# An attention and MLP kernel on one core: the last batch's first MLP product by a seven-product scheme, variances by ScalarE squares, and a new order

## The chip, the core and the metric

One NeuronCore of a Trainium2 chip. The kernel is one program, launched once, with inputs and output in HBM. The metric is the device time of an execution in microseconds; the median of several runs counts. TensorE (PE) multiplies, VectorE (DVE), ScalarE (ACT) and GpSimd (POOL) do the elementwise work, and SyncE's queue (SP) issues nearly all transfers. TensorE writes to PSUM, eight banks of 512 fp32 columns in 128 partitions; GpSimd works on SBUF alone.

## The reference

Four batches of 768 positions, eight heads of 64. The first half is a causal block-sparse attention; the second mixes its output and runs an MLP:

```python
# attention, per batch and head (S = 768, D = 64, blocks of 64 keys)
k_rep = mean of k over each block                     # 12 blocks
gate  = q @ k_rep.T, causal by block                   # S x 12
sel   = top 3 blocks of gate, and the own block
attn  = softmax(q @ k.T / 8 over the selected, causal) # S x S
x     = attn @ v                                       # heads side by side: 768 x 512

# mixing and MLP, per batch
X     = fft(fft(x, axis=seq), axis=model)
u     = x + real(X)
un    = (u - mean(u)) / sqrt(var(u) + 1e-6)            # over the 512 columns
ch    = relu(un @ w_ch1) @ w_ch2                       # 512 -> 2048 -> 512
out   = u + ch
```

## The kernel before

The work is cut into some 1160 steps, and one hand-written string, `ORDER`, lists them. Each word is a step, `name:arguments@place`; a tilde ahead of it picks the other of two engines. A loop at the end goes through the words and emits each step's instructions; nothing is reordered after that. Each engine therefore runs its own instructions in the order of the list and waits by semaphores for its inputs. `@place` names the buffer that a step's result takes, above all one of four PSUM slots of two banks each.

Attention runs over 16 pairs of heads (pair P belongs to batch P // 4): loads `Lq`, `Lk`, `Lv`, scores `s` (six tiles a pair), exponentials `e` on ACT, causal masks `d` on POOL, `v` (probabilities times values) on TensorE, the normalised result `x` on DVE. Then, per batch: folds `fs`, `fd`, `f`, `fe` (they halve the transforms), the first transform `y` with its copies `ty` and `tr`, the second transform `m`, and `u`, which adds x on DVE and collects the row sums (`m_u`).

Per batch and tile of 128 rows follow the statistics, the normalising and the transpose:

- `bn` (`n_stats`, lines 747 and 748): bn_stats over 512 columns and bn_aggr, on DVE;
- `nv` (`n_guess`): a first guess of 1/sqrt of the variance, on DVE, for two tiles at a time; `nr` (`n_newton`): Newton steps in small POOL instructions;
- `xu` (`m_x`, lines 704 and 707): centring and scaling to fp16, one tile on ACT and one on DVE;
- `un` (`t_copy`, line 742): two transposing transfers on SP's queue, which put the two tiles into `unT`. Later `od` steps (line 832, results to HBM) share this queue.

The MLP's first product is `w` (`w1_mm`, lines 801 and 803): sixteen steps a batch, each with four weight tiles of 128 x 128 against 768 columns of `unT`, as 512 and 256. `r` (`w1_relu`, lines 811 and 813) takes the relu of all 768 columns from PSUM to fp16 `hT`, on ACT or DVE.

The second product is plain for batches 0 and 1 (`c`, line 820, with `o` at line 826). For batches 2 and 3 (`W7`) it is already a seven-product scheme: instead of eight products of half matrices it forms seven of sums of halves. `T` (`w2_comb`) builds four sums of w2's quarters; `S` (`h_comb`) four sums of the quarters of `hT`, 32 steps a batch, 128 x 384 fp16, through the helper `tt` at line 250; `p` (`w7_mm`, line 879) is one product for 128 rows, eight matmuls of 256 columns; `po` (`w7_o`, line 886) scales the partial result and adds it to u on DVE. Seven products in three row groups make 21 `p` and 21 `po` a batch. Partial products that go to the same place are added up in the PSUM bank, which each `po` reads in between.

The order at the end before the change: `c` of batch 1 interleaved with the scores of pairs 14 and 15; `w:2`; the transforms of batch 3 in between; `p:2`, then `w:3`, then `p:3` and the last `od`.

Of the kernel before, what the change touches and what calls it, by code (L numbers as in the profile page):

```python
# [19 lines left out]
S = 768  # L20
# [84 lines left out]

ORDER = """
# [24 lines left out]
Lv:7@1 bn:0,1 r:0,0 s:7,1@3 Lk:10@0 r:0,10 ks:9 d:7,3 w:0,11@0 e:7,1 qc:8@1 s:7,2@1 kh:9 ~r:0,11  # L131
# [25 lines left out]
e:13,2 gl:14 s:13,4@2 f:2,2 w:1,3@0 ~fe:2,0 e:13,4 gm:14@2 d:13,2 ~fe:2,3 f:2,3 d:13,1 kh:15
w:1,14@3 f:2,1 r:1,7 K:14 qc:15@1 s:12,4@2 r:1,14 ~fe:2,2 f:2,0 w:1,0@1 e:12,4 nv:1 s:13,0@3 fe:2,1
~r:1,3 y:2,0@2 e:13,0 ~r:1,0 d:13,0 s:12,2@0 d:13,3 pg:2 g:15@3 e:12,2 d:13,4 y:2,1@1 gt:15 vc:13
tr:2,0 d:12,0 s:12,3@3 Lv:14@0 gu:15 nr:1 gx:15 ty:2,0 c:1,0,0@0 go:15 gl:15 e:12,3 ~ty:2,1 v:13@2  # L160
~tr:2,1 ~qs:15 m:2,0@3 d:12,3 x:13 d:12,2 qs:14 m:2,2@1 gm:15@3 kc:15 u:2,0@0 c:1,1,0 d:12,4 d:12,5
bn:2,0 vc:12 s:14,1@2 u:2,2@2 s:14,0@3 K:15 c:1,0,1 e:14,0@0 bn:2,4 e:14,1 bn:2,1 s:14,2@1 d:14,0
bn:2,5 s:14,4@3 e:14,2 c:1,1,1 e:14,4 ~vc:14 v:12@2 o:1,1 o:1,0 od:1,1 s:15,0@1 nv:2,2 od:1,0
s:15,5@3 c:1,4,0@0 e:15,5@1 e:15,0 xu:2,2 x:12 d:15,0 s:15,3@3 d:14,2 s:14,3@1 nv:2,0 un:2,2 e:15,3
c:1,4,1 fs:13,1 e:14,3 xu:2,0 d:15,3 fs:13,0 d:14,4 s:14,5@2 d:14,1 m:2,1@3 o:1,4 e:14,5 d:15,5
s:15,1@1 od:1,4 u:2,1@1 d:14,3 s:15,2@2 e:15,1 c:1,5,0 bn:2,2 e:15,2 d:15,1 d:14,5 bn:2,3 s:15,4@3
d:15,2 v:14@1 nv:2,1 e:15,4 ~xu:2,1 c:1,5,1 d:15,4 un:2,1 nr:2 v:15@2 o:1,5 T:2 od:1,5 c:1,2,0@3
un:2,0 x:14 c:1,2,1 x:15 fs:12,1 fs:12,0 c:1,3,0 fs:14,1 fs:14,0 fs:15,1 fs:15,0 fd:14,1 fd:15,1
# [28 lines left out]
def kernel(  # L197
# [546 lines left out]

    def n_stats(b, kt):
        bst = spool.tile([128, 6], FP, tag="bst", name=f"bst{kt}_{b}", bufs=4)
        nc.vector.bn_stats(out=bst, in_=u_t[b, kt // 2][:, kt % 2, :])
        nc.vector.bn_aggr(out=st_t[b][0][:, kt, :], in_=bst)

    def n_guess(b, kp=None):  # L750
        if b in W7:

            if len(st_t[b]) == 3:
                st_t[b].append([spool.tile([128, NST], FP, tag=n, name=f"{n}_{b}")
                                for n in ("vr", "t2")])
            k = slice(2 * kp, 2 * kp + 2)
            mv, g, nm, vr = [t[:, k] for t in (*st_t[b][0:3], st_t[b][3][0])]
# [6 lines left out]
            nc.vector.scalar_tensor_tensor(out=nm, in0=mv[:, :, 0], scalar=-1.0, in1=g,  # L764
                                           op0=ALU.mult, op1=ALU.mult)
# [68 lines left out]
    w2t, h_s, rt_t = [], {}, {}  # L834

    def w2_comb(n):
        if not w2t:
            w2t.extend(apool.tile([128, PT_W], F16, tag=f"pt{m}", name=f"w2t{m}", bufs=1)[:, 0:4096]
                       .rearrange("p (n i c) -> p n i c", n=2, c=256) for m in range(2))
        lo, hi = slice(0, 256), slice(256, 512)  # L840
        for i0, i1 in ((0, 8),):
            b11, b21, b12, b22 = [w2_sb[:, r + i0:r + i1, c] for c in (lo, hi) for r in (0, 8)]
            t = [w2t_at(m, i0, i1) for m in range(4)]
            in0, in1 = ((b12, b11), (b22, t[0]), (b22, b12), (b21, t[1]))[n]
            tt(t[n], in0, in1, ALU.subtract)

    def w2t_at(m, i0, i1):
        return w2t[m // 2][:, m % 2, i0:i1, :]

    def h_comb(b, i, n):  # L850
# [5 lines left out]
        def a(r, c):  # L856
            return h_t[b, i + 8 * (c - 1)][:, 384 * (r - 1):384 * r]
# [3 lines left out]
        tt(s[:, n, :], in0, in1, ALU.subtract if n else ALU.add)  # L861

    def w7_mm(b, n, st):
# [86 lines left out]
    def ind_slot0():  # L950
# [61 lines left out]
```

## Time and profile before

| | |
|---|---|
| Runs | 277.74, 280.2, 277.95 us; median 277.95 |
| Profiled execution | 277.79 us, its span 276.1 us |
| Granted TensorE clock | 1.00 |
| TensorE busy | 267.9 us (97%), 2660 matmuls |
| VectorE busy | 221.5 us (80%), 683 instructions |
| ScalarE busy | 178.3 us (65%), 243 |
| GpSimd busy | 107.4 us (39%), 304 |
| Read from HBM, written | 28.55 MB, 6.29 MB |

The span runs from the first to the last instruction; the execution's own time is 1.7 us longer. Rows of groups give the code line, engine, operation, result and inputs with shape and type, the number, and behind the first bar the busy time and the mean duration of one instruction in ns; behind the second bar stands the idle time of the engine just ahead of them and what ended it. Rows of the timeline give start and duration in us. A waiting row reads "who waited <- for whom: us in total, times, longest". Matmuls are pipelined, so a row's duration is longer than its distance to the next one; distances are the better price. Names such as `L801` are the lines of the kernel above; `L250` and `L239` are helpers that many steps share.

### The profile page before, as it was taken

The page shows a single profiled execution, that of the slowest core. Times are in us where ns is not written, and L with a number is a line of the kernel's source. Part 1 is how long each engine was busy: PE and PEld are TensorE (multiplying, and loading weights), DVE is VectorE, ACT ScalarE, POOL GpSimd, SP SyncE. Part 2 cuts the span into 40 slices and gives each one's busy share as a digit, 9 for nine tenths or more (in the row PEclk, how much of TensorE's full clock was granted, in tenths as well). Part 3 has the DMA queues.
Part 4 walks back from the last instruction along what each step waited for, and adds up shares of the span by engine and source line. Part 5 has one row for each costly group of instructions (what it writes and reads, how often), then busy time and mean ns, then how long its engine had stood idle before and what let it go on. Part 6 is the DMA issues. An engine that isn't in the chain of part 4 may idle for free.

```text
span 276.1 us, 7004 instructions
## 1 busy us (share of the span) xinstructions
PE 267.9 (97%) x2660; PEld 181.2 (66%) x2660; DVE 221.5 (80%) x683; ACT 178.3 (65%) x243; POOL 107.4 (39%) x304
## 2 busy tenths in 40 slices
PE   8899989999999999999999999999999999999995
PEld 4566766765576565666665755655766888666884
DVE  1888999998789889899789797879999894307883
ACT  3799999969999759978799687802546310274100
POOL 5155927634783476405976691520100011000000
PEclk9999999999999999999999999999999999999999
DMA  8999999998799999479471202351100412300025
GB/s 190 271 229 235 186 233 207 180 153 151 134 174 189 168 188 194 115 124 234 119 149 29 57 2 78 77 105 51 38 2 0 59 19 68 127 0 2 0 112 194
DMA packets 121138, 33.47 MB, mean 121 GB/s; under 512 B 113616, under 2 KB 118160, under 8 KB 121104
## 3 DMA queue, kind: packets, MB, share of 16 engines
q1 hardware_dynamic: 115872, 28.43, 48.1%
q0 software_dynamic: 3664, 4.19, 9.8%
q10 hardware_dynamic: 1568, 0.39, 0.6%
q8 instruction: 21, 0.34, 0.5%
q14 instruction: 13, 0.11, 0.1%
HBM read 28.55 MB, written 6.29 MB: 126 GB/s over the span
## 4 chain that ended last, share of the span: by engine, by line
PE 81%; DVE 6%; ACT 5%; POOL 2%; issue 2%; SPq 2%; DMA 1%; DVEq 0%; ACTq 0%; POOLq 0%
PE h L801 19%; PE cw L879 13%; PE c L820 12%; PE h L803 9%; PE sc L532 7%; PE av L567 5%; PE tp L320 2%; ACT pt L549 2%; PE yp L639 2%; PE sc L527 2%; PE mx L672 2%; SPq L742 2%; PE mx L673 2%; PE sc L539 1%; PE warmps L914 1%
## 5 line engine op out<-in xcount | busy, mean ns | idle before, releaser
L549 ACT ACTIVATE pt<-sc 128x1024 f16<-128x1024 f32 (+1 forms) x96 | 83.4, 925 | 12.1 <-PE sc L532 8.1
L801 PE MATMUL h<-unT,w 128*128 128x512 f16 x256 | 84.6, 379 | 0.3 <-DMA unT<-x 0.3
L803 PE MATMUL h<-unT,w 128*128 128x256 f16 x256 | 69.7, 272 | 0.0
L813 ACT ACTIVATE hT<-h 128x768 f16<-128x768 f32 x50 | 39.4, 811 | 41.1 <-PE h L803 40.7
L555 POOL TENSOR_SCALAR_AFFINE_SELECT pt<-pt 128x256 f16<-128x256 f16 x96 | 37.4, 413 | 21.0 <-ACT pt L549 19.9
L820 PE MATMUL c<-w_sb,hT 128*128 128x512 f16 x192 | 44.5, 379 | 0.0
L801 PEld LDWEIGHTS <-w 128*128 128x128 f16 x256 | 25.0, 98 | 29.7 <-issue 1.4
L820 PEld LDWEIGHTS <-hT 128*128 128x128 f16 x192 | 18.3, 98 | 20.3 <-issue 0.5
L253 POOL TENSOR_SCALAR_AFFINE_SELECT qk<-mt 32x160 f16<-32x160 f16 x72 | 23.9, 353 | 18.2 <-DVE mt L504 16.7
L803 PEld LDWEIGHTS <-w 128*128 128x128 f16 x256 | 25.0, 98 | 3.6
L532 PE MATMUL sc<-qk 96*128 96x512 f16 (+3 forms) x144 | 26.1, 305 | 0.0
L567 PEld LDWEIGHTS <-pt 128*128 128x128 f16 x672 | 22.3, 97 | 3.2 <-ACT pt L549 0.7
L567 PE MATMUL av<-v,pt 128*128 128x65 f16 x672 | 23.2, 193 | 0.3 <-ACT pt L549 0.3
L253 POOL TENSOR_SCALAR_AFFINE_SELECT qk<-q 64x768 f16<-64x768 f32 (+1 forms) x15 | 12.3, 822 | 22.8 <-ACT q L239 15.3
L886 DVE SCALAR_TENSOR_TENSOR u<-cw,rt,u 128x256 f32<-128x256 f32 x35 | 16.6, 480 | 4.7 <-PE cw L879 4.1
L879 PEld LDWEIGHTS <-s 128*128 128x128 f16 x192 | 18.8, 98 | 2.2
L532 PEld LDWEIGHTS <-qk 96*128 96x128 f16 x144 | 13.1, 98 | 7.8
L811 DVE TENSOR_SCALAR hT<-h 128x768 f16<-128x768 f32 x14 | 13.3, 956 | 4.0 <-PE h L803 3.9
L879 PE MATMUL cw<-w2t,s 128*128 128x256 f16 x144 | 16.4, 273 | 0.0
L250 DVE TENSOR_TENSOR s<-hT,hT 128x384 f16<-128x384 f16 x16 | 5.4, 354 | 13.4 <-ACT hT L813 13.3
L250 DVE TENSOR_TENSOR x<-av,rcp 128x768 f16<-128x768 f32 x16 | 15.3, 958 | 0.6
L879 PEld LDWEIGHTS <-hT 128*128 128x128 f16 x144 | 14.1, 98 | 2.0
(155 smaller groups left out, 457.2 us busy)
## 6 DMA issues: line engine op xcount, KB each, us to landing
nat<-in_v_dram SPq DMA_DIRECT2D x16, 384.0 KB, 4.6
out_dram<-u SPq DMA_DIRECT2D x20, 256.0 KB, 2.4
nat<-in_k_dram SPq DMA_DIRECT2D x36, 96.0 KB, 3.4
nat<-in_q_dram SPq DMA_DIRECT2D x36, 96.0 KB, 2.9
nat<-in_q_dram SPq DMA_DIRECT2D x13, 192.0 KB, 3.7
nat<-in_k_dram SPq DMA_DIRECT2D x13, 192.0 KB, 3.9
w_sb<-in_moe_w_ch_dram POOLq DMA_DIRECT2D x2, 1024.0 KB, 11.2
w<-in_moe_w_ch_dram POOLq DMA_DIRECT2D x2, 768.0 KB, 7.1
```

What stands on the lines that cost most here:

```text
L250: (eng or nc.vector).tensor_tensor(out=out, in0=in0, in1=in1, op=op)
L253: nc.gpsimd.affine_select(out=out, in_=in_, pattern=[[0, i] for i in n], base=0, channel_multiplier=0, compare_op=ALU.is_ge, fill=0.0)
L532: nc.tensor.matmul(ps[:, e, co:co + q1 - q0], qk[0:96, e, 1, 128 * jt:128 * jt + 128], qk[0:96, e, 0, q0:q1], start=True, stop=True)
L549: nc.scalar.activation(out=d["pt"][:, o:o + 2 * n].rearrange("p (e c) -> p e c", e=2), in_=d["sc", i][:, :, 0:n], func=AF.Exp, scale=0.125)
L555: nc.gpsimd.affine_select(out=dg, in_=dg, pattern=[[0, 2], [1, 128]], base=0, channel_multiplier=-1, compare_op=ALU.is_ge, fill=0.0)
L567: nc.tensor.matmul(av[:, e, 66 * st:66 * st + 65], pt[:, co:co + 128], vv[:, e, jt, 0:65], start=(cnt == 0), stop=(cnt == 20))
L801: nc.tensor.matmul(hp[:, 0:512], w1s, unT[:, dt, 0:512], start=(dt == 0), stop=(dt == NDT - 1))
L803: nc.tensor.matmul(hp[:, 512:768], w1s, unT[:, dt, 512:768], start=(dt == 0), stop=(dt == NDT - 1))
L813: nc.scalar.activation(out=hT, in_=hp, func=AF.Relu)
L820: nc.tensor.matmul(c_ps[b, g[0]][:, st - g[0], :], h_t[b, it][:, 128 * st:128 * (st + 1)], w2_sb[:, it, :], start=(it == 0), stop=(it == N ...
L879: nc.tensor.matmul(o, x, y, start=(i == 0 and W7_FIRST[n]), stop=(i == 7), skip_group_check=True)
L886: nc.vector.scalar_tensor_tensor(out=o, in0=c_ps[b, "w", st][:, W7_BANK[n], 0:256], scalar=rt_t[b][:, kt:kt + 1], in1=o, op0=ALU.mult, op1 ...
```

## The change

Three things change.

First, batch 3's first product. `unT` is split into halves of its contraction (two pairs of 128-row tiles) and of its columns (384 each), w1 into halves of its contraction and of its 2048 outputs. `W6 = 3` names the batch. `wa` (`w6_comb`) builds four sums of w1's quarters in twelve pieces, on DVE or POOL, in buffers of the attention that are free by then; `ub` (`w6_tcomb`) four sums of the quarters of `unT` on DVE. Then, for eight groups i of outputs, seven products `k:i,n` (`w6_mm`), each two matmuls of 384 columns into one of two banks of a PSUM slot. The sums wander through PSUM: `zc` (`w6_keep`) copies the first bank's partial sum to SBUF in fp32 three times (ACT or DVE), `za` (`w6_add`) adds the second bank and such a copy on DVE into an fp32 tile, `zm` (`w6_max`) takes its relu to fp16 on POOL or ACT, and `zr` (`w6_relu`) takes the first bank's last state directly. Sixteen `w`, sixteen `r` of 768 columns become 56 `k`, 24 `zc`, 24 `za`, 24 `zm` and 8 `zr` of 384.

Second, the statistics of batches 2 and 3: `mn` turns the row sums into negative means on DVE, `sq` lets ACT square u minus the mean and collect the sum, and `nv` takes the variance from that. The twelve `bn` of these batches fall away.

Third, the order from the end of batch 0's output on is new, engines included: a few `S` and the `wa` go to POOL (tilde), copies and relus change sides, the first `k` stand among the last `p:2`, and the first `p:3` among the last `k`. Ahead of that place one neighbouring pair of steps on different engines is exchanged. In `w7_mm`, `w7_o` and `h_comb` the row halves of batch 3 are taken the other way round (`half`).

```diff
+W6 = 3
+W6_A = ((0, 2), (2, 4), (4, 8))
...
+    def n_mean(b, kp):
+        sm = st_t[b][2][:, 2 * kp:2 * kp + 2]
+        nc.vector.tensor_scalar(out=sm, in0=sm, scalar1=-1.0 / DM, scalar2=None, op0=ALU.mult)
+
+    def n_square(b, kt):
+        nc.scalar.activation(out=x_t[b][:, kt, :], in_=u_t[b, kt // 2][:, kt % 2, :], func=AF.Square,
+                             bias=st_t[b][2][:, kt:kt + 1], accum_out=st_t[b][0][:, kt, 1:2])
...
-            nc.vector.tensor_scalar(out=vr, in0=mv[:, :, 1], scalar1=1e-6, scalar2=None, op0=ALU.add)
+            nc.vector.tensor_scalar(out=vr, in0=ss, scalar1=1.0 / DM, scalar2=1e-6, op0=ALU.mult, op1=ALU.add)
...
-            nc.vector.scalar_tensor_tensor(out=nm, in0=mv[:, :, 0], scalar=-1.0, in1=g,
-                                           op0=ALU.mult, op1=ALU.mult)
+            tt(nm, nm, g, ALU.mult)
...
+    def w6_comb(n, r):
...
+        in0 = (lambda: a(1, 0), lambda: w6_sum(0, i0, i1), lambda: a(0, 0), lambda: a(0, 1))[n]()
+        in1 = (lambda: a(1, 1), lambda: a(0, 0), lambda: a(1, 0), lambda: w6_sum(1, i0, i1))[n]()
+        tt(w6_sum(n, i0, i1), in0, in1, ALU.subtract if n else ALU.add, pick(nc.vector, nc.gpsimd))
...
+    def w6_tcomb(n):
+        in0 = (lambda: w6_b(0, 1), lambda: w6_b(1, 1), lambda: w6_b(1, 1), lambda: w6_b(1, 0))[n]()
+        in1 = (lambda: w6_b(0, 0), lambda: w6_t(0), lambda: w6_b(0, 1), lambda: w6_t(1))[n]()
+        tt(w6_t(n), in0, in1, ALU.subtract)
...
+    def w6_mm(i, n):
+        if (i, "p") not in w6:
+            w6[i, "p"] = pst([128, 2, 512], f"k{i}_{W6}")
+        o = w6[i, "p"][:, W7_BANK[n], 0:384]
...
+        for d in range(2):
+            nc.tensor.matmul(o, x[:, d, :], y[:, d, :], start=(d == 0 and W7_FIRST[n]), stop=(d == 1),
+                             skip_group_check=True)
+
+    def w6_keep(i, j):
+        conv(pick(nc.scalar, nc.vector), w6_copy(i, j), w6[i, "p"][:, 0, 0:384], None)
+
+    def w6_relu(i):
+        hp, h = w6[i, "p"][:, 0, 0:384], w6_h(i, 1, 0)
+        if pick(0, 1):
+            nc.vector.tensor_scalar(out=h, in0=hp, scalar1=0.0, scalar2=None, op0=ALU.max)
+        else:
+            nc.scalar.activation(out=h, in_=hp, func=AF.Relu)
+
+    def w6_add(i, j):
+        tt(w6_tmp(i, j), w6[i, "p"][:, 1, 0:384], w6_copy(i, (0, 2, 1)[j]), ALU.add)
+
+    def w6_max(i, j):
+        h, t = w6_h(i, *((0, 0), (1, 1), (0, 1))[j]), w6_tmp(i, j)
+        if pick(0, 1):
+            nc.scalar.activation(out=h, in_=t, func=AF.Relu)
+        else:
+            nc.gpsimd.tensor_scalar(out=h, in0=t, scalar1=0.0, scalar2=None, op0=ALU.max)
...
-            tt(t[n], in0, in1, ALU.subtract)
+            tt(t[n], in0, in1, ALU.subtract, pick(nc.vector, nc.gpsimd))
...
-        tt(s[:, n, :], in0, in1, ALU.subtract if n else ALU.add)
+        tt(s[:, n, :], in0, in1, ALU.subtract if n else ALU.add, pick(nc.vector, nc.gpsimd))
```

The order around the new product, cut:

```diff
+S:2,6,1 po:2,1,1 p:2,1,2 po:2,1,0 S:2,5,1 xu:3,2 p:2,2,1 un:3,2 S:2,2,2 po:2,1,2 p:2,2,0 ...
+p:2,3,2 S:2,6,2 ub:2 k:0,0@2 S:2,3,3 k:0,1 po:2,3,2 p:2,3,1 S:2,5,3 zc:0,0 S:2,4,3 po:2,3,0 p:2,4,2
+za:0,0 po:2,3,1 ~zm:0,0 p:2,4,0 wa:1,2 p:2,4,1 ...
+... k:1,0@0 zc:2,0 p:2,5,0 za:2,0 k:0,6 po:2,5,0 k:2,2 za:0,1 k:1,1 zc:2,1 p:2,6,0 zc:1,0 zm:0,1 zr:0
+za:1,0 k:2,3 k:2,5 po:2,6,0 k:1,2 zm:1,0 ~zc:2,2 od:2,3 k:0,4 ~wa:2,2 zc:1,1 k:3,0@1 ...
+k:6,6 za:4,2 ~zm:3,2 k:7,2 zm:7,0 k:5,6 za:6,1 zc:7,1 p:3,0,2@2 zm:4,2 za:5,1 zr:6 S:3,3,0 zr:5 k:7,3
+S:3,3,2 ~zm:5,1 k:7,5 S:3,4,0 po:3,0,2 k:6,4 zc:7,2 ~S:3,4,1 k:5,4 za:6,2 k:7,6 ...
```

More of the change, by code (lines that the diff above doesn't have):

```diff
@@ L157 @@
[L157 to L168, printed above, removed]
@@ L836, in w2_comb, with w2t_tiles @@
+    w2t, w2p, h_s, rt_t = [], [], {}, {}
+    def w2t_tiles():
+        if not w2p:
+            w2p.extend(apool.tile([128, PT_W], F16, tag=f"pt{m}", name=f"w2t{m}", bufs=1)
+                       for m in range(2))
+            w2t.extend(t[:, 0:4096].rearrange("p (n i c) -> p n i c", n=2, c=256) for t in w2p)
     def w2_comb(n):
-        if not w2t:
-            w2t.extend(apool.tile([128, PT_W], F16, tag=f"pt{m}", name=f"w2t{m}", bufs=1)[:, 0:4096]
-                       .rearrange("p (n i c) -> p n i c", n=2, c=256) for m in range(2))
+        w2t_tiles()
@@ L844, in w2_comb, with half @@
             in0, in1 = ((b12, b11), (b22, t[0]), (b22, b12), (b21, t[1]))[n]
-            tt(t[n], in0, in1, ALU.subtract)
+            tt(t[n], in0, in1, ALU.subtract, pick(nc.vector, nc.gpsimd))
     def w2t_at(m, i0, i1):
         return w2t[m // 2][:, m % 2, i0:i1, :]
+    def half(b, r):
+        return 1 - r if b == W6 else r
     def h_comb(b, i, n):
@@ L866, in w7_mm @@
         o = c_ps[b, "w", st][:, W7_BANK[n], 0:256]
-        rows, low = slice(128 * st, 128 * st + 128), slice(128 * (st + 3), 128 * (st + 4))
+        rows, low = [slice(128 * k, 128 * k + 128) for k in (st + 3 * half(b, 0), st + 3 * half(b, 1))]
         lo, hi = slice(0, 256), slice(256, 512)
@@ L883, in w7_o @@
         r, c = W7_OUT[n]
-        kt = st + 3 * r
+        kt = st + 3 * half(b, r)
         o = u_t[b, kt // 2][:, kt % 2, 256 * c:256 * c + 256]
```

144 lines of the change are left out of this document (109 added, 35 removed).

## The prediction

> **What bounds the kernel now.** I read the page's head and its forty slices first, then TensorE's own waits from 120 us on, then busy time by stretch.
>
> ```profile
> span 276.1 us, 7004 instructions
> PE 267.9 (97%) x2660; PEld 181.2 (66%) x2660; DVE 221.5 (80%) x683; ACT 178.3 (65%) x243; POOL 107.4 (39%) x304
> PE   8899989999999999999999999999999999999995
> ```
>
> ```profile
> PE av L567 <- ACT pt L549: 0.3, 1, 0.3
> PE h L801 <- DMA unT<-x: 0.3, 1, 0.3
> ```
>
> ```profile
> 134.50:214.29 79.79, 79.22 (x715) 50.42 (x713) 68.59 (x203) 50.53 (x67) 32.46 (x89) 1.00 0.25 59
> 214.29:233.50 19.21, 19.21 (x178) 17.21 (x176) 15.57 (x44) 2.62 (x4) 2.54 (x11) 1.00 0.27 43
> 233.50:250.00 16.50, 16.50 (x104) 9.92 (x102) 2.62 (x4) 7.57 (x10) 0.00 (x0) 1.00 0.17 64
> 250.00:276.10 26.10, 22.80 (x196) 18.95 (x194) 19.01 (x53) 2.55 (x4) 0.00 (x0) 1.00 0.23 82
> ```
>
> In the windows the columns are PE, PEld, DVE, ACT, POOL, the granted clock (1.00), DMA. The order list changes in earnest only from about 134.5 us on (the steps listed behind that place are 138.3 us of TensorE, counted back from the last drain at 272.8 us, which the chain further down shows). From there TensorE has no gap but two of 0.3 us and the 3.3 us behind its last matmul. So the kernel is TensorE's column count, and any column taken out after 134.5 us is time, as long as the other engines follow. Between 233.5 and 250 us they are nearly idle: DVE 2.6 of 16.5 us, ACT 7.6, POOL nothing. That stretch is the last batch's first product, which is what the change replaces.
>
> **What is removed.** The price of a column comes from two neighbouring rows of TensorE's timeline: 24 matmuls of 256 columns from 230.88 to 233.50.
>
> ```profile
> 230.88 2.78 PE L879 MATMUL cw<-w2t,hT 128*128 128x256 f16 x24
> 233.50 0.38 PE L801 MATMUL h<-unT,w 128*128 128x512 f16 x1
> ...
> L532 PE MATMUL sc<-qk 96*128 96x512 f16 x54 | 14.9, 379 | 0.0
> L532 PE MATMUL sc<-qk 96*128 96x256 f16 x36 | 5.2, 272 | 0.0
> L532 PE MATMUL sc<-qk 96*128 96x384 f16 x18 | 4.3, 325 | 0.0
> ```
>
> 2.62 us for 6144 columns, 0.109 us for each matmul. The scores' rows show that 384 columns stand in the middle between 256 and 512 (325 against 272 and 379 ns), so width has no step there. Sixteen w steps of 4 x 768 columns are 49,152 columns; fifty-six k steps of 2 x 384 are 43,008. The difference is again 6144 columns: **2.62 us**. A k step takes 0.327 us, the whole product 18.3 instead of 20.9 us. Nothing else on TensorE changes but order.
>
> **What is added, and what hides it.** Durations and the spacing of queued instructions:
>
> ```profile
> L250 DVE TENSOR_TENSOR x<-av,rcp 128x768 f16<-128x768 f32 x16 | 15.3, 958 | 0.6
> L250 DVE TENSOR_TENSOR ltb<-gt,mx 128x120 f16<-128x120 f32 x9 | 2.7, 301 | 1.1 <-POOL gt L495 1.0
> L886 DVE SCALAR_TENSOR_TENSOR u<-cw,rt,u 128x256 f32<-128x256 f32 x35 | 16.6, 480 | 4.7 <-PE cw L879 4.1
> ...
> 256.76 0.48 DVE L886 SCALAR_TENSOR_TENSOR qk<-cw,rt,qk 128x256 f32<-128x256 f32 x1
> 257.16 0.48 DVE L886 SCALAR_TENSOR_TENSOR u<-cw,rt,u 128x256 f32<-128x256 f32 x1
> 261.89 0.62 DVE L250 TENSOR_TENSOR s<-hT 128x384 f16<-128x384 f16 x2
> ```
>
> A queued drain (po) starts 0.40 us behind the one before although it lasts 0.48, and two half-sums (S) take 0.62: queued instructions overlap by about 0.08 us. An addition za (384 fp32, one input in PSUM) lies on the line from 301 ns (120) to 958 (768): 0.57 us, 0.49 queued. Twenty-four are 11.6 us of DVE.
>
> ```profile
> L239 ACT CAST qk<-tp 128x512 f16<-128x512 f32 x1 | 0.6, 587 | 0.8 <-DVE kra L390 0.8
> L239 ACT CAST qk<-tpj 128x256 f16<-128x256 f32 x1 | 0.4, 377 | 0.0
> 171.59 1.94 ACT L549 ACTIVATE pt<-sc 128x1024 f16<-128x1024 f32 x2
> L549 ACT ACTIVATE pt<-sc 128x1024 f16<-128x1024 f32 x80 | 78.5, 1032 | 8.2 <-PE sc L532 5.8 <-POOL v L253 0.8 <-PE sc L539 0.6
> ```
>
> A copy zc out of PSUM (384) is half way between 377 and 587: 0.48 us; two exponentials of 1.03 in 1.94 us give an overlap of 0.1, so 0.39 queued. Between k:1,0 and k:5,4 the list gives TensorE 47 k and 3 p steps, 18.0 us; ACT 34 instructions (19 zc, 6 zr, 9 zm), 13.3 us queued and 16.3 unqueued; DVE 19 za, 9 S, 3 po and 3 reads of PSUM taken at 0.5, 9.3 + 2.4 + 1.2 + 1.5 = 14.4 us. Both fit, ACT at 74 to 91% and DVE at 80%. I take the queued figures, since these queues stand full. What is late when za comes late: the slot's next k step, and behind it on TensorE, which keeps its order, the other slots' k steps and the p steps among them; so the cover is the other three slots' work, and without it every za would cost its 0.57 us and two hops.
>
> ```profile
> L253 POOL TENSOR_SCALAR_AFFINE_SELECT qk<-q 128x768 f16<-128x768 f32 x5 | 4.1, 825 | 15.3 <-ACT q L239 15.3
> L907 POOL TENSOR_SCALAR_AFFINE_SELECT id<-wid 128x128 f32<-128x128 f32 x1 | 0.3, 292 | 0.1
> 180.14 0.20 POOL L250 TENSOR_TENSOR t<-vr,rt 128x6 f32<-128x6 f32 x1
> 180.41 0.20 POOL L250 TENSOR_TENSOR t<-t,rt 128x6 f32<-128x6 f32 x1
> ```
>
> POOL's relu zm of 384 lies between 292 and 825: 0.5 us. A POOL half-sum or weight combination has no wide row; I bound it by the one-input line (0.5 us for 384, 1.04 for 1024) and twice that, and take the upper end. The first p:3 step needs zm:7,0. From zm:0,1 to it POOL has 8 zm, 3 S, one 1024-wide wa and nr:3 (11 small ones 0.28 apart, 3.1 us): 9.6 to 12.2 us, against 41 k steps, p:2,6,0 and seven eighths of p:3,0,2, which are 15.0 us of TensorE. It fits.
>
> [...]
>
> The 4 ub and DVE's 7 wa (fp16, at most 0.7 us each, since an S of 384 takes 0.35) come before the k stage, at most 7.7 us, where the removed statistics free more. TensorE's last 22.8 us hold 21 po, 23 S and 9 za, 8.4 + 6.2 + 4.4 = 19.0 us of DVE: as much as it did in that stretch before (19.0) without holding TensorE. I take nothing for these.
>
> **Variances.**
>
> ```profile
> L747 DVE BATCH_NORM_STATS2 bst<-u 128x6 f32<-128x512 f32 x22 | 14.8, 674 | 0.0
> L748 DVE BATCH_NORM_AGGREGATE mv<-bst 128x2 f32<-128x6 f32 x24 | 4.4, 182 | 0.8
> L704 ACT ACTIVATE x<-u,sm,rs 128x512 f16<-128x512 f32 x5 | 4.0, 809 | 10.3 <-DVE sm L764 10.3
> L691 DVE DVE_READ_ACCUMULATOR u<-mx,x 128x1 f32 x22 | 1.8, 82 | 0.0
> ```
>
> Twelve pairs of 0.86 us leave DVE (10.3 us), twelve squares of 0.81 (plus a read of the accumulator, between nothing and 0.2) go to ACT: 9.7 to 12 us. ACT was busy 50.5 of 79.8 us up to 214.3, so the mean allows it. Behind sq:2,5 and sq:2,0 on ACT's queue stand the exponentials of pairs 14 and 15, whose PSUM slots the next s steps need; a square late by a DVE mean delays them. Bounds 0 to 1.5 us (two squares in a row); I take 0, because six squares are 5 us in some 25.
>
> **The transposes.** The chain of waits shows what they cost:
>
> ```profile
> 180.38 1.22 SPq L742
> ...
> 182.27 2.52 SPq L742
> 184.84 2.50 DMA unT<-x
> 187.47 0.38 PE h L801
> ...
> 272.84 0.48 DVE qk L886
> ...
> unT<-x SPq DMA_TRANSPOSE x18, 2.5
> nat<-in_v_dram SPq DMA_DIRECT2D x16, 384.0 KB, 4.6
> ```
>
> Today un:2,0 stands on SP behind od:1,5, and TensorE waits 0.3 us. The new order puts un:2,1 last but ahead of od:1,5: that 0.3 us goes. New is a tight place: k:0,0 needs un:3,2 inside p:2. From the end of p:2,1,0 to k:0,0 lie six p steps (6 x 0.873 = 5.2 us); the chain is the wait and po (0.6), S (0.27), xu (0.54), the second issue (1.2) and the landing (2.5): 5.1 us. Bounds: nothing to 1.3 us, when DVE is two instructions late; I take 0.3. Behind k:0,0 on TensorE stand k:0,1 and the last ten p:2 steps, and DVE's po wait for those. The loads that change places on SP (Lv:12 to Lv:14, one transfer each, and Lq:15, four) keep 6 us or more of TensorE work between issue and use, against 4.6 us to land: nothing.
>
> **Slots.** In the k stage a PSUM slot lives through five k steps in a chain with zc, zc, zc, za, za. A hop is 0.2 us (a p step ends at 231.75, its drain starts at 231.96):
>
> ```profile
> 231.96 0.48 DVE L886 SCALAR_TENSOR_TENSOR u<-cw,rt,u 128x256 f32<-128x256 f32 x1 [0.39 <-PE cw L879]
> ```
>
> 5 x (0.33 + 0.2) + 3 x 0.58 + 2 x 0.67 = 5.7 us. Four slots serve eight chains, so the stage is held only when a turn exceeds 18.3 / 2 = 9.1 us, that is when each of the five hand-overs queues 0.7 us. Bounds 0 to 3 us; I take 0.3.
>
> **The sum.** Profiled execution 277.79 (span 276.1 and 1.7 around it), less 2.62, less the two waits of 0.3, plus 0.3 and 0.3: 275.2. The median of the runs shown is 277.95, 0.16 above it: **275.3 us**, 0.95% less.
>
> **Rivals.**
> 1. *Partial loss.* A turn takes 9.5 to 10.7 us: the stage is 19 to 21.4 us, the gain shrinks to nothing: 276.2 to 278.5. For it: three in-order engines at 75 to 90%. Against it: in the last 26 us DVE ran as full and TensorE never waited.
> 2. *Slower.* Place: the same stage. From a turn of 9.1 us it decides; from 11.9 us (1.2 us queued at each hand-over) the kernel is over 1% slower. At 12.5 us the stage takes 25 us: 277.95 - 2.62 + 6.7 = 282. For it: nr:3 alone blocks POOL's relus 3.1 us. Against it: no rate in the rows is that slow.
> 3. *It does not save.* If 384 columns cost 512, 112 x 0.218 = 24.4 us against 20.9: 281.5. The 384 row speaks against it.
>
> **Numbers.** Forecast, 274.3 to 276.2: 0.64, of which 0.36 below 275.17. Partial loss: 0.18. Slower: 0.15, no saving 0.03, nearly all above 280.7. One per cent, about what a measurement of this kernel can tell from no change, is 2.8 us: faster 0.36, same 0.46, slower 0.18. The range 274.3 to 280.0 leaves out the slow cases. The forecast alone: 274.3 to 276.2.
>
> **What would show it.** TensorE's matmuls 2644, their busy time near 265; waits of k steps on ACT or DVE below 1 us in sum; k:0,0 waiting for the transpose under 0.5; zc rows near 480 ns, za near 570, sq near 810, zm on POOL near 500. It is wrong if k or p:3 steps wait over 2 us in all, if POOL rows reach 1 us for a relu, or if exponentials late behind squares show as TensorE waits before 190 us.

## The result, and the profile after

The changed kernel takes 280.75 us (median of 13 runs, 280.37 to 283.51), the kernel before 277.95 (13 runs beside it). The ratio is 1.0108, 95% interval 1.0082 to 1.0134: slower by 2.8 us, where 275.3 was forecast with a range up to 280.0. The columns were saved, and more than they were worth came back as waits in the new product and behind the last matmul.

The head of the page after, with TensorE's and GpSimd's slices:

```profile
span 281.0 us, 7100 instructions
PE 267.0 (95%) x2644; PEld 179.6 (64%) x2644; DVE 230.8 (82%) x692; ACT 194.3 (69%) x296; POOL 133.5 (48%) x328
PE   8899989899999999999999999999999999978993
POOL 5165918524784476406975771530532000988100
```

Sixteen matmuls fewer, as the scheme says. TensorE's busy time fell by 0.9 us only, to 267.0 and not near 265: the end of a row is modelled (a k step's row lasts 0.49 us where the next one can start 0.33 us after it), so part of every gap counts as busy, and the text goes by the distances of rows. TensorE's row now has a dent (7, 8) in slices 36 and 37, from 246 to 260 us, and GpSimd's row shows 9, 8, 8 in slices 35 to 37. This profiled execution took 282.69 us, 1.9 above the median of its kernel; 1.6 us of that were lost before 131 us, in code that did not change, and belong to this execution alone. The same scores, first in the kernel before and then in the changed one, and the start of p:2 in the latter (214.29 before):

```profile
131.01 0.28 PE L532 MATMUL sc<-qk 96*128 96x128 f16 x2
```

```profile
132.63 0.28 PE L548 MATMUL sc<-qk 96*128 96x128 f16 x2
...
217.01 0.38 PE L1014 MATMUL cw<-w_sb,hT 128*128 128x256 f16 x2
```

So the profiled difference, 282.69 - 277.79 = 4.90 us, splits into stretches. Up to 131 us: +1.62. From there to p:2: 2.72 - 1.62 = +1.10, of which 0.87 is the transform step m:3,2 that now stands ahead of p:2 instead of inside it; the rest is gaps of the new order (0.24 us ahead of y:2,0, 0.24 ahead of v:13, 0.13 at a score), less the 0.43 at the transpose that the kernel before waited for. From the start of p:2 to the start of the last drain (276.53, shown below): 59.52 against 58.55, +0.97. That stretch has lost m:3,2 (0.87) and the 6144 columns (2.62), so 0.97 + 0.87 + 2.62 = 4.5 us of gaps are new in it. Behind the start of the last drain: 4.47 against 3.26, +1.21.

TensorE's waits from 120 us on, then two of DVE's, in the changed kernel (the last of TensorE's, for an exponential, stands in the kernel before too):

```profile
PE k L939 <- DVE w L266: 1.8, 1, 1.8
PE cw L1014 <- POOL hT L960: 0.8, 1, 0.8
PE cw L1014 <- DVE w_tr L266: 0.3, 1, 0.3
PE av L583 <- ACT pt L565: 0.3, 1, 0.3
```

```profile
DVE w L266 <- POOL hT L960: 2.2, 1, 2.2
DVE s L266 <- POOL hT L960: 1.3, 1, 1.3
```

The largest wait is named after DVE, and DVE itself was waiting for GpSimd. The timeline shows the hand-over:

```profile
248.20 0.49 PE L939 MATMUL k<-uns,qk 128*128 128x384 f16 x2
...
248.71 1.16 POOL L960 TENSOR_SCALAR hT<-w 128x384 f16<-128x384 f32 x1
...
249.91 0.56 DVE L266 TENSOR_TENSOR w<-k,w 128x384 f32<-128x384 f32 x1 [2.19 <-POOL hT L960]
...
250.52 0.48 PE L939 MATMUL k<-uns,qk 128*128 128x384 f16 x2 [1.83 <-DVE w L266]
```

za:6,0 is to write the fp32 tile that zm:4,0 on GpSimd has still to read (`w6_area(i % 2)`: groups 4 and 6 share it). DVE keeps its order, so the additions of the other slots stand behind za:6,0, and TensorE stops at k:6,2, which waits for it. The second wait is p:3,0,2 for zm:7,0. Busy time by stretch, PE, PEld, DVE, ACT, POOL, first before, then after:

```profile
240.00:250.00 10.00, 10.00 (x64) 6.00 (x62) 0.16 (x1) 5.94 (x8) 0.00 (x0) 1.00 0.00 0
250.00:260.00 10.00, 10.00 (x81) 7.72 (x80) 9.06 (x28) 2.55 (x4) 0.00 (x0) 1.00 0.01 2
```

```profile
240.00:250.00 10.00, 8.69 (x52) 4.87 (x50) 6.75 (x15) 7.43 (x17) 9.90 (x10) 1.00 0.22 80
250.00:260.00 10.00, 8.32 (x56) 5.33 (x56) 8.06 (x21) 6.40 (x15) 8.28 (x17) 1.00 0.00 0
```

From 240 to 250 us GpSimd is the fullest engine, 9.9 of 10 us, where it had nothing to do before. The groups that the prediction had priced, by shape:

```profile
L939 PE MATMUL k<-uns,qk 128*128 128x384 f16 x48 | 10.2, 326 | 1.8 <-DVE w L266 1.8
L960 POOL TENSOR_SCALAR hT<-w_tr 128x384 f16<-128x384 f32 x4 | 4.9, 1222 | 0.4 <-DVE w_tr L266 0.4
L960 POOL TENSOR_SCALAR hT<-w 128x384 f16<-128x384 f32 x3 | 3.5, 1163 | 0.0
L266 POOL TENSOR_TENSOR s<-s,hT 128x384 f16<-128x384 f16 x5 | 4.6, 915 | 3.6 <-DVE s L266 3.6
L266 POOL TENSOR_TENSOR qk<-w,w 128x1024 f16<-128x1024 f16 x1 | 2.1, 2120 | 0.0
L255 ACT COPY w<-k 128x384 f32<-128x384 f32 x17 | 8.0, 479 | 18.0 <-PE k L939 17.8
L266 DVE TENSOR_TENSOR w_ty<-k,w 128x384 f32<-128x384 f32 x6 | 3.3, 552 | 0.5 <-ACT hT L950 0.2 <-PE k L939 0.2
L766 ACT ACTIVATE x<-u,sm 128x512 f16<-128x512 f32 x10 | 7.1, 713 | 2.7 <-DVE sm L763 2.6
L766 ACT ACTIVATION_READ_ACCUMULATOR x<-u,sm 128x1 f32 x10 | 1.9, 188 | 0.0
```

A maximum on GpSimd takes 1.16 to 1.22 us, not 0.5. (The 326 ns of the first row are the duration of one matmul. A k step has two, and by the distance of its rows, nine steps from 240.36 to 243.29 us, it takes 0.326 us.) The end, from the chain of waits and from SP's queue:

```profile
276.53 0.48 DVE qk L1021
```

```profile
273.57 3.51 SPq L855 DMA_DIRECT2D out_dram<-u  x4
277.18 0.41 SPq L855 DMA_DIRECT2D out_dram<-qk  x1
277.69 0.39 SPq L855 DMA_DIRECT2D out_dram<-u  x1
278.17 0.41 SPq L855 DMA_DIRECT2D out_dram<-qk  x1
```

The last drain ends at 277.01; its transfer is issued 1.16 us later, since SP's queue is still busy with earlier issues (before: 0.03 us later).

### The profile page after: what moved, and what is told of

Read it like the earlier page. It is cut to its first block, busy times and chain, and to the rows that moved or that the text cites. A ratio compares the mean times of both kernels' runs of the same rounds, so it can differ in the third digit from the quotient of the medians.

```text
span 281.0 us, 7100 instructions
## 1 busy us (share of the span) xinstructions
PE 267.0 (95%) x2644; PEld 179.6 (64%) x2644; DVE 230.8 (82%) x692; ACT 194.3 (69%) x296; POOL 133.5 (48%) x328
## 4 chain that ended last, share of the span: by engine, by line
PE 69%; POOL 9%; DVE 9%; ACT 8%; issue 4%; POOLq 0%; DVEq 0%; ACTq 0%
PE c L843 15%; PE cw L1014 12%; PE h L824 10%; PE sc L548 6%; PE av L583 6%; PE h L826 5%; POOL hT L960 4%; ACT pt L565 3%; PE tp L336 2%; PE yp L655 2%; DVE u L707 2%; ACT x L766 2%; PE sc L543 2%; ACT hT L836 2%; POOL qk L269 1%
## 5 line engine op out<-in xcount | busy, mean ns | idle before, releaser
L824 PE MATMUL h<-unT,w 128*128 128x512 f16 x192 | 63.7, 379 | 0.0
L826 PE MATMUL h<-unT,w 128*128 128x256 f16 x192 | 52.3, 272 | 0.0
L571 POOL TENSOR_SCALAR_AFFINE_SELECT pt<-pt 128x256 f16<-128x256 f16 x96 | 38.0, 421 | 18.6 <-ACT pt L565 11.5
L824 PEld LDWEIGHTS <-w 128*128 128x128 f16 x192 | 18.7, 97 | 21.7 <-issue 0.7
L269 POOL TENSOR_SCALAR_AFFINE_SELECT qk<-mt 32x160 f16<-32x160 f16 x72 | 23.1, 342 | 18.9 <-DVE mt L520 17.5
L836 ACT ACTIVATE hT<-h 128x768 f16<-128x768 f32 x35 | 27.5, 808 | 6.2 <-PE h L826 6.1
L826 PEld LDWEIGHTS <-w 128*128 128x128 f16 x192 | 18.8, 98 | 3.0
L255 ACT COPY w<-k 128x384 f32<-128x384 f32 x17 | 8.0, 479 | 18.0 <-PE k L939 17.8
L707 DVE SCALAR_TENSOR_TENSOR u<-mx,x 128x512 f32<-128x512 f32 x22 | 14.1, 681 | 3.6 <-DMA out_dram<-u 2.7
L543 PE MATMUL sc<-qk 64*128 64x512 f16 (+3 forms) x112 | 14.9, 306 | 1.6 <-DVE u L707 1.0
```

The source lines that it names most:

```text
L269: nc.gpsimd.affine_select(out=out, in_=in_, pattern=[[0, i] for i in n], base=0, channel_multiplier=0, compare_op=ALU.is_ge, fill=0.0)
L543: nc.tensor.matmul(ps[:, e, co:co + q1 - q0], qk[hs[e], 1, XW(P), 128 * jt:128 * jt + 128], qk[hs[e], 0, XW(P), q0:q1], start=(co == 0), s ...
L571: nc.gpsimd.affine_select(out=dg, in_=dg, pattern=[[0, 2], [1, 128]], base=0, channel_multiplier=-1, compare_op=ALU.is_ge, fill=0.0)
L707: nc.vector.scalar_tensor_tensor(out=u_b[:, k2, :].rearrange("p (m two) -> p two m", two=2), in0=mps[:, k2, :].rearrange("p (two m) -> p t ...
L824: nc.tensor.matmul(hp[:, 0:512], w1s, unT[:, dt, 0:512], start=(dt == 0), stop=(dt == NDT - 1))
L826: nc.tensor.matmul(hp[:, 512:768], w1s, unT[:, dt, 512:768], start=(dt == 0), stop=(dt == NDT - 1))
```

## The experiments

Theory: GpSimd's list (maxima at 1.17 us, sums at 0.92) holds the k stage. Rival: the serial turn of a PSUM slot through three engines does, whatever GpSimd's share. Four runs went first. The kernel before had medians of 277.56, 277.89, 277.95 and 277.68 us beside the four groups of runs, so each kernel is given as its median and as its distance from the one before next to it; the changed kernel stands at +2.80.

**e1: maxima from GpSimd to ScalarE.** All ten:

```diff
-zm:0,1 ... zm:1,0 ... zm:5,2
+~zm:0,1 ... ~zm:1,0 ... ~zm:5,2
```

> The ten relus zm on GpSimd go to ScalarE; all else is as in the changed kernel (280.75 us). Theory GpSimd: its relu of 384 fp32 takes 1.17 us, not the 0.5 of the sum, so GpSimd is busy without a gap from 238.9 to 258.6 us and the k and p:3 steps wait 3 to 4 us for it. Then GpSimd loses 11.7 us of work in that stretch, the waits go, and the time is 276.8 to 277.8. Rival turn (a PSUM slot's round of copies and sums is too long whatever engine does the relu): ScalarE gets ten more instructions of 0.52 us, the waits stay at 3 us or more, 280 or above.

280.03 us, +2.5 (ratio 1.0094, 1.0069 to 1.0118). Almost nothing is won: the theory's time is missed, and the rival's is met. In the trace TensorE still loses 2.7 us in the k stage, and ScalarE is now busy for 9.4 of 10 us from 240 us on.

**e2: sums from GpSimd to VectorE.** The five S:3 and wa:2,2:

```diff
-~S:3,0,0 ... ~S:3,0,1 ... ~wa:2,2
+S:3,0,0 ... S:3,0,1 ... wa:2,2
```

> The five half-sums S:3 and the weight combination wa:2,2 on GpSimd go to VectorE; the relus stay on GpSimd. Theory GpSimd: 5 x 0.92 + 2.1 = 6.7 us leave GpSimd's full stretch of 19.7 us, VectorE gets 5 x 0.27 + 0.6 = 2 us; the relus come some us earlier and most of the waits go: 277.3 to 278.8. Rival VectorE (VectorE, 8 of 10 us busy there, is what k waits for): 2 us more on it make it slower, 281 to 283.

279.79 us, +2.2 (1.0082, 1.0061 to 1.0102). Also a miss, between the two ranges.

**e3: both.** 

> Both: GpSimd keeps only the Newton steps there. Theory GpSimd: as the relus alone or a little better, 276.5 to 277.8. Rival turn or VectorE: 280 or above, since ScalarE and VectorE now carry everything.

279.64 us, +2.1 (1.0089, 1.0058 to 1.0120), again between the two ranges. With GpSimd empty the waits of 1.8 and 0.8 us are gone, yet TensorE still loses 2.9 us from 240 to 255, in pieces of 0.04 to 0.46. Its windows show where the work went (PE, PEld, DVE, ACT, POOL):

```profile
240.00:245.00 5.00, 4.53 (x27) 2.36 (x26) 3.95 (x10) 4.68 (x12) 0.00 (x0) 1.00 0.24 87
245.00:250.00 5.00, 4.71 (x27) 2.43 (x26) 3.93 (x12) 4.89 (x13) 0.00 (x0) 1.00 0.00 0
250.00:255.00 5.00, 4.75 (x29) 2.68 (x28) 4.76 (x13) 5.00 (x13) 0.00 (x0) 1.00 0.00 0
```

ScalarE is now the full engine, 14.6 of 15 us, and its copies zc stand behind maxima. The theory "GpSimd alone" falls; the stage is short of draining time on whichever engine gets the maxima.

**e4: one output transfer earlier.**

```diff
-... od:2,5 ... po:3,5,2 od:2,4 od:3,0,1 ...
+... od:2,4 od:2,5 ... po:3,5,2 od:3,0,1 ...
```

> The output transfer od:2,4 stands ahead of od:2,5 instead of between the last transfers of batch 3. In the changed kernel the end lies 4.7 us behind the last matmul, against 3.5 us before, and one of the last transfers took 2.05 us to issue. Theory queue: a transfer less stands ahead of the last one, and the tail shrinks by 0.4 to 1.2 us: 279.5 to 280.4. Rival: the long issue comes from elsewhere, and the time stays at 280.5 to 281.

280.18 us, +2.6 (1.0089, 1.0067 to 1.0111). The time is in the theory's range. In its profile the last drain ends at 274.62 and the last transfer is issued at 274.68:

```profile
271.18 2.43 SPq L854 DMA_DIRECT2D out_dram<-u  x3
273.71 0.38 SPq L854 DMA_DIRECT2D out_dram<-qk  x1
274.18 0.41 SPq L854 DMA_DIRECT2D out_dram<-u  x1
274.68 0.41 SPq L854 DMA_DIRECT2D out_dram<-qk  x1
```

The span ends 3.1 us behind the last drain instead of 4.0; in the median only some 0.2 us can be seen, where the theory said 0.4 to 1.2.

**e5: e3 and e4 together.** 

> GpSimd freed of sums and maxima as in e3, and the whole-row transfer od:2,4 issued ahead of od:2,5 as in e4. In the profile of e3 the last transfer is issued 1.1 us after its po has ended, in that of e4 0.06 us after. Theory queue (SyncE's own list, not the compute engines, sets the last microsecond): the two gains add, 279.64 - 0.9 = 278.7 (278.4 to 279.1). Rival (the tail is the time of the transfers themselves, not of their issue): no gain over e3, 279.4 to 279.9.

279.14 us, +1.25 (1.0050, 1.0034 to 1.0066): 0.8 less than e3 against the kernels beside them, though the intervals touch. In the profile of e5 the span ends 3.7 us behind the last drain (e3: 4.0), since its last transfer still goes out 0.9 us late: three issues ahead took 3.26 us there and 2.43 in e4. That SP's list makes the tail is supported, the size of what this move brings is not settled.

**e6: no maxima at all.** `za` writes h, the 24 `zm` are left out, so that three quarters of h lack their relu:

```diff
-        tt(w6_tmp(i, j), w6[i, "p"][:, 1, 0:384], w6_copy(i, (0, 2, 1)[j]), ALU.add)
+        tt(w6_h(i, *((0, 0), (1, 1), (0, 1))[j]), w6[i, "p"][:, 1, 0:384], w6_copy(i, (0, 2, 1)[j]), ALU.add)
```

> Leaves out the 24 zm steps (the maxima with zero of three quarters of the last batch's first product); za writes straight into h. Theory drain (the k stage is held by the engines that empty PSUM and make h, not by TensorE): 11.9 us of GpSimd and 7.3 us of ScalarE go, the waits of 1.8, 0.8 and 0.3 us go, time 277.3 to 278.4. Rival turn (the serial path of a slot, k to zc to k to za to k, sets the pace): the maxima are no part of that path, time 279.3 or more.

278.29 us, +0.4 (1.0018, 1.0003 to 1.0034). The maxima are worth 2.4 us; the serial turn without them is not what holds the stage. Its trace loses 0.6 us in the k stage and 1.1 at p:2,1,1 (see e8).

**e7 and e7b: squares and order without the new product.** w:3, r:3 and the tail of before behind the changed order up to p:2:

```diff
-... ub:2 k:0,0@2 ... zc ... za ... zm ... k:7,6 ...
+... od:2,4 w:3,5@2 ... r:3,15 ... p:3,6,0 ...
```

> The changed kernel without the seven-product scheme: w:3 with r:3 and the tail in the order of before, no wa, ub, k, zc, za, zm, zr; squares and the new order up to p:2 stay. Theory (squares and order cost nothing, the loss is all in the k stage and the tail): 276.6 to 277.6, at most at the time of before. Rival (squares or the new order cost): 278.3 or more.

279.12 us, +1.2 (1.0044, 1.0026 to 1.0063). My splice had put two p:2 steps of one slot side by side, which cost 0.74 us in the trace. e7b has before's order there.

> As e7 (no seven-product scheme; squares and the new order up to p:2), with the last p:2 steps in the order of before. In the profile of e7 TensorE lost 0.74 us behind p:2,5,0, where two steps of one slot stood next to each other (my splice), and 0.3 us at p:2,1,1. Theory (squares and order cost at most 0.3 us): 279.12 - 0.74 = 278.4 or less, 277.9 to 278.5. Rival (squares and order cost a microsecond by something else): 278.8 or more.

278.40 us, +0.45 (1.0027, 1.0006 to 1.0049). Squares and order are not free, but nearly: 0.3 us of it, by the distance of TensorE's rows, is one stall at p:2,1,1. TensorE's rows show two more new gaps, 0.24 us ahead of y:2,0 (151.66) and 0.23 ahead of v:13 (155.38). Both stand ahead of the first square, so the order makes them and not the squares, and together they take back the 0.43 of the removed wait. The view of waits in e7b names the stall:

```profile
PE cw L1005 <- DVE u L1012: 0.2, 1, 0.2
```

**e8: ten maxima on VectorE, in fp16.** za as in e6, and zm in place:

```diff
-        h, t = w6_h(i, *((0, 0), (1, 1), (0, 1))[j]), w6_tmp(i, j)
+        h = t = w6_h(i, *((0, 0), (1, 1), (0, 1))[j])
-            nc.gpsimd.tensor_scalar(out=h, in0=t, scalar1=0.0, scalar2=None, op0=ALU.max)
+            nc.vector.tensor_scalar(out=h, in0=t, scalar1=0.0, scalar2=None, op0=ALU.max)
```

> za writes its sum in fp16 straight into h, and the ten maxima that GpSimd made are made in place by VectorE, fp16 to fp16 (taken at 0.25 to 0.4 us each from the 0.35 us of a two-input fp16 sum of that size); sums stay on GpSimd. Theory drain: GpSimd loses 11.9 us, VectorE gains 2.5 to 4: 278.6 to 279.6. Rival turn: VectorE's list becomes longer, and the turn with it: 280 or more.

278.63 us, +0.7 (1.0018, 0.9985 to 1.0051): 2.1 us less than the changed kernel, with everything still computed. This also does away with the fp32 tile that two groups share; e10 tells the two apart. The ten maxima cost VectorE 3.4 us where they cost GpSimd 11.9:

```profile
L960 DVE TENSOR_SCALAR hT<-hT 128x384 f16<-128x384 f16 x10 | 3.4, 337 | 0.0
```

The trace has a new stall of 0.9 us at p:2,1,1, and its cause is in the two engines' timelines:

```profile
212.54 2.12 POOL L266 TENSOR_TENSOR qk<-w,w 128x1024 f16<-128x1024 f16 x1
...
212.60 2.35 DVE L723 TENSOR_SCALAR x<-u,rs,sm 128x512 f16<-128x512 f32 x1
```

Without maxima ahead of it in GpSimd's list, wa:2,2 starts at 212.5 instead of 241 us, and the VectorE instruction that began 0.06 us later took 2.35 us where the same form takes 0.54 elsewhere; it ended 0.29 us after GpSimd's. The same pair stands in e1 and e6 (2.36 us of VectorE beside 2.13 of GpSimd), where the stall is 0.9 us too, and explains part of e1's miss. Why VectorE takes longer beside GpSimd's sum is not shown by these rows.

**e9: e8 with wa:2,2 on VectorE and od:2,4 early.** (The edit of e4 for od:2,4, and:)

```diff
-... k:0,4 ~wa:2,2 zc:1,1 ...
+... k:0,4 wa:2,2 zc:1,1 ...
```

> e8 (za writes fp16 into h, the ten maxima of GpSimd in place on VectorE) with wa:2,2 on VectorE instead of GpSimd and od:2,4 ahead of od:2,5. In the profile of e8 one TENSOR_SCALAR of VectorE took 2.35 instead of 0.54 us while GpSimd's wa:2,2 ran, and TensorE lost 0.9 us at p:2,1,1 behind it. Theory (three places hold the loss: GpSimd's maxima, the two engines shutting each other out, SyncE's list at the end): 278.63 - 0.9 - 0.5 = 277.2 (276.7 to 277.6), under the kernel before. Rival (VectorE, 9.6 and 9.9 of 10 us busy in the k stage, is the bound, and what it takes over comes back as waits): 278.2 or more.

277.86 us, -0.1 (0.9999, 0.9978 to 1.0020): 0.8 less than e8 rather than 1.4. The loss is gone, and the saving still does not show. In its profile the stall at p:2,1,1 is down to 0.3 us and the span ends 2.9 us behind the last drain.

**e10: as e8, but the maxima stay on GpSimd, fp16 to fp16.** (Only the `tt` and `h = t` lines of e8.)

> As e8, but the ten maxima stay on GpSimd, in place, fp16 to fp16. Theory A (GpSimd's 1.17 us is the price of the fp32 source): 0.6 us or less each, time 279 to 279.8. Theory B (it is the price of the operation by element, whatever the type): 1.1 to 1.2 us each, time 280.2 to 281.

282.36 us, +4.4 (1.0172, 1.0128 to 1.0215). The price is theory B's, whatever the type, but the time is above both:

```profile
L960 POOL TENSOR_SCALAR hT<-hT 128x384 f16<-128x384 f16 x10 | 11.8, 1192 | 25.8 <-DVE hT L266 25.8
```

```profile
PE cw L1014 <- POOL hT L960: 3.1, 1, 3.1
```

```profile
253.90:254.05 0.15, 0.00 (x0) 0.00 (x0) 0.15 (x2) 0.00 (x0) 0.15 (x1) 1.00 0.00 0
254.10:254.30 0.20, 0.00 (x0) 0.00 (x0) 0.20 (x1) 0.00 (x0) 0.20 (x1) 0.50 0.00 0
255.20:260.90 5.70, 5.70 (x23) 3.26 (x23) 3.17 (x8) 2.43 (x5) 3.06 (x3) 0.50 0.01 3
261.00:264.00 3.00, 3.00 (x29) 2.60 (x27) 2.56 (x8) 0.52 (x1) 0.91 (x1) 1.00 0.00 0
```

The shared tile is gone, and with it the k stage's 1.8 us. The delay now lands on p:3,0,2 as a whole: 3.1 us there, against 1.8, 0.8 and 0.3 in the changed kernel. So the tile had chosen the place of the delay, and GpSimd's list its size. The granted clock (third column from the end) falls at 254.1 us, 2.1 us after TensorE's last matmul ended, and is back at 1.00 at 260.9. Between the end of the wait and then TensorE's rows stand up to twice as far apart, which costs 2.8 us in this execution. The mean granted clock was 0.986 to 0.991 in all four executions of e10, against 0.996 or more in those of e8, enough to account for a time above theory B. Against e8, which differs in the engine of ten maxima alone, it is 3.7 us.

**e11: e9 with the five S:3 on VectorE.** (Tildes off, as in e2.)

> e9 with the five half-sums S:3 of GpSimd on VectorE too, so that nothing wide runs on GpSimd in the k stage. VectorE gains 5 x 0.35 = 1.8 us and loses about 1 us of being shut out (four instructions of 0.24 to 0.34 us took 0.50 to 0.60 beside GpSimd's sums in e8). Theory (the shut-outs cost as much as the sums): within 0.4 us of e9. Rival (VectorE is the bound): 0.6 to 1 us above e9.

278.85 us, +0.9 (1.0032, 1.0002 to 1.0063), 1.0 above e9, though the intervals touch: the rival. In the profiles 0.6 us of it lie between the start of p:2 and the last matmul. So more work on VectorE costs time in the relieved stage, and GpSimd's slow sums are worth having.

Three more experiments ask what squares and order cost, and what paces the stage once GpSimd is relieved.

**e12: e9 with VectorE's wait moved.** In e9's timeline VectorE stands 0.93 us in nv:3,2 for ScalarE's last square, and po:2,0,1, which p:2,1,1 needs, is queued behind:

```profile
216.43 0.17 DVE L782 TENSOR_SCALAR vr<-mv 128x2 f32<-128x2 f32 x1 [0.93 <-ACT x L765]
```

```diff
-... un:3,0 nv:3,2 p:2,0,0@1 ... po:2,1,1 ...
+... un:3,0 p:2,0,0@1 ... po:2,1,1 nv:3,2 ...
```

> e9 with nv:3,2 behind po:2,1,1 on VectorE, so that po:2,0,1 no longer stands behind VectorE's wait of 0.9 us for ScalarE's last square. Theory (that wait is the stall of 0.3 us at p:2,1,1): the stall goes, 277.86 - 0.3 = 277.5 (277.2 to 277.7). Rival (another instruction of VectorE is late as well): no change, 277.8 to 278.1.

277.76 us, +0.1 (1.0006, 0.9989 to 1.0024): the rival's time. The stall at p:2,1,1 is gone, so nv:3,2 and its wait for the last square were its cause, but 0.13 us come back ahead of p:2,1,0, and 0.37 inside p:2,2,1 (221.24), where TensorE waits for a half-sum of VectorE.

**e13: e12 with three maxima on ScalarE.**

```diff
-zm:3,1 ... zm:4,2 ... zm:5,2
+~zm:3,1 ... ~zm:4,2 ... ~zm:5,2
```

> e12 with the maxima zm:3,1, zm:4,2 and zm:5,2 on ScalarE (0.52 us each, ScalarE 5.7 of 10 us busy from 250 to 260 in e8) instead of VectorE (0.24 to 0.5 us each, 9.9 of 10 busy). Theory (VectorE paces the end of the k stage): 0.2 to 0.5 us under e12. Rival (the serial path of a slot paces it): within 0.15 us of e12 or above it.

278.17 us, +0.5 (1.0013, 0.9997 to 1.0029): the rival's side, not clear of noise. The windows of e12, then e13:

```profile
250.00:260.00 10.00, 9.93 (x80) 7.60 (x78) 9.93 (x29) 5.90 (x14) 2.03 (x3) 1.00 0.01 2
```

```profile
250.00:260.00 10.00, 9.86 (x78) 7.43 (x76) 9.32 (x26) 6.84 (x17) 2.06 (x3) 1.00 0.01 2
```

VectorE has 0.6 us more room and TensorE no more work done. VectorE's rate alone no longer sets the stage there.

**e14: e9 with the old statistics.** `sq` becomes `bn`, `mn` goes, `nv` as before.

```diff
-mn:3,0 mn:3,1 ... sq:3,1 ... sq:3,4
+bn:3,1 ... bn:3,4
```

> e9 with the statistics of batches 2 and 3 by bn_stats and bn_aggr on VectorE, as in the kernel before, at the places of the squares; no mn, no squares on ScalarE. My prediction's step (squares cost nothing): within 0.3 us of e9 if VectorE has the room, so 277.6 to 278.2. Rival A (VectorE has no room for 12 x 0.9 us of statistics there, which is what the squares bring): 278.5 to 280. Rival B (the squares cost): 277.5 or less.

281.97 us, +4.3 (1.0131, 1.0093 to 1.0169). Rival A, and more than it said:

```profile
PE cw L1014 <- DVE u L1021: 3.4, 1, 3.4
```

```profile
221.10:224.50 3.40, 3.40 (x17) 2.35 (x17) 1.95 (x6) 0.05 (x1) 0.00 (x0) 0.51 0.41 83
```

In the changed order VectorE has no room for ten microseconds of statistics ahead of p:2. From the end of the wait on the granted clock is at one half for 3.4 us, and TensorE's rows lose another 1.6 us by it. The two executions with a mean granted clock of 0.997 and 0.998 took 280.86 and 279.91 us, the three with 0.991 and 0.992 took 281.97 to 282.89. This is the value of the squares in this order, not in that of before.

## Why the prediction was wrong, by its own steps

The forecast for a profiled execution was 275.17 us. Gaps behind p:2's start were 4.5 us where 0.6 was taken (+3.9), the stretch ahead of p:2 came out 0.2 longer where 0.6 was to go (+0.8), and the end 1.2 longer where nothing was taken: 281.1. The other 1.6 us belong to this execution.

- *The columns*: right. A k step takes 0.326 us, and 2.62 us of TensorE's work are gone by count and distance; the busy time near 265 did not come (267.0).
- *zc, za, squares*: right in size: 0.48, 0.55 and 0.71 + 0.19 us against 0.48, 0.57 and 0.81 with up to 0.2.
- *The relu zm on POOL*: the step that failed first. I read 0.5 us off a line through two rows of another operation, affine_select; it is 1.17 us. So "It fits" was wrong, and a wait that the sum had at nothing came to 3.0 us (1.8, 0.8 and 0.3). From zm:0,1 (238.88) to the end of zm:7,0 (256.10) GpSimd's list is 17.2 us long, not 9.6 to 12.2, and longer than the 15.0 us that TensorE has beside it. The POOL sums, taken at the upper end, were right (0.92 and 2.12 us). "POOL rows reach 1 us for a relu" and waits "over 2 us in all" were among my signs of being wrong; both came.
- *Slots, 0.3 us*: mis-sized. The gaps behind p:2's start were 4.5 us in the changed kernel, 3.0 of them the waits just named. The maxima's place accounts for most (e8, e10); with the maxima off GpSimd some 1.4 us of k hand-overs stay (e9: pieces of 0.03 to 0.28 us). I had the serial chain, 5.7 us a turn, and the mean loads, 74 to 91%, and took the one as a proof that the other would not queue. In e9 VectorE is busy for 9.3 and ScalarE for 9.1 of the 10 us from 240 us on, and TensorE still loses 0.8 us there: engines that keep an order fixed in advance hold each other up before the mean is full. I had also left out that two groups share an fp32 tile, which turned a late engine into a stop of the other slots.
- *The transposes*: right. TensorE loses 0.2 us ahead of k:0,0, by the distance of its rows, against 0.3 us taken, and the old wait for a transpose is gone.
- *The other wait of 0.3 us taken off*: wrong. It is the wait for an exponential, for whose going the prediction gave no reason, and it stands in the changed kernel as before.
- *The variances at nothing*: nearly. Squares and order alone stand 0.45 us above the kernel before (e7b), though the removed wait should have put them below; two new gaps of the order, ahead of y:2,0 and v:13, took that back. 0.3 us is the stall at p:2,1,1, which e12 ties to nv:3,2 and its wait for the last square; that m:3,2, now ahead of p:2, had been its cover is an inference. I had followed the squares to the exponentials, not to nv and the drain queued behind it.
- *The end*: not in my sum at all. The new list has seven issues behind one another on SP's queue from 273.57 us on, and the tail is 1.2 us longer in the profile. I had counted SP's issues for the loads and transposes, not for the last `od`.
- *Rivals*: "slower" had the right stage, but the wrong mechanism: it needed no turn of 11.9 us, since one late engine stopped the other slots at once and the end added its part; that the time, 280.75, lies where this rival begins is luck; against it I had written that no rate in the rows is that slow, with no row of that operation to say so.

What stays open: the 1.4 us of small hand-overs in e9. With 0.5 us ahead of p:2,1,1 and k:0,0 and 0.6 of gaps in the new order before p:2, less the 0.4 of the removed wait, they use up 2.1 of the 2.6 us that the scheme saves. e11 makes them worse with more work on VectorE and e13 no better with less, so VectorE's load is a part and its order against ScalarE's another; they were not separated. e9 and the kernel before are equal within 0.2%.

## What to carry to other kernels

When a change swaps matrix work for elementwise work, price each new operation on the very engine it is given to; where no row has it, let its bound decide the range and not a neighbour's line. Add up the list of each engine between the first and the last consumer in that stage, treat every engine whose list comes near the matrix engine's as a bound, and every tile shared by two groups as a place where one late engine stops the rest. And follow the last output transfers through their queue whenever the final order is rewritten: 1.2 us hid there in the profile that no compute engine showed.

## What the runs showed of the hardware that was not expected

- GpSimd's one-input maximum (1.16 to 1.22 us for 384 elements, the same 1.19 from fp16) is slower than its two-input fp16 sum of that size (0.92).
- Beside a wide GpSimd sum of 2.12 us a VectorE instruction took 2.35 us where it takes 0.54 elsewhere (e8). The two-input form of VectorE is hit too, here even though it began first. From the changed kernel, a half-sum that takes 0.35 us elsewhere, beside a 512-wide wa on GpSimd:

```profile
200.22 1.47 DVE L266 TENSOR_TENSOR s<-hT,hT 128x384 f16<-128x384 f16 x1
```

```profile
200.32 1.15 POOL L266 TENSOR_TENSOR qk<-w,w 128x512 f16<-128x512 f16 x1
```

- What a wait of TensorE cost in these runs depended on the granted clock behind it. A wait of 1.8 us left it at 1.00 (changed kernel). In e10 it fell 2.1 us into a wait of 3.1 and stayed at 0.50 for 6.8 us, which cost another 2.8 us; in e14 it fell as a wait of 3.4 ended and stayed there for 3.4 us, which cost another 1.6. What sets the moment of the fall and the length of the low stretch is not shown.
